# GateLoop attention and a max-out FFN on one core: FFN steps given out whole, none of them between the turn and the cut

## Chip, cores and metric

One core of a Trainium2 chip runs the kernel. The metric is the device time in microseconds (us) of one execution, and the median over several executions is what is compared. Beside it, one execution is recorded by the hardware profiler, which gives a trace of every instruction. TensorE is called PE below, VectorE DVE, ScalarE ACT, GpSimd POOL and SyncE SP, as in the profile.

## What is computed

Two blocks follow each other. The first is attention with a complex gate for each channel (4 batches, 8 heads, 768 positions, 48 channels for each head), written as a recurrence over positions. The second is a feed-forward network over the 3072 tokens that takes the largest of three products.

```python
mag = np.sqrt(a_re * a_re + a_im * a_im)
scale = np.minimum(mag, 0.999) / (mag + 1e-06)
a_re_n, a_im_n = (a_re * scale, a_im * scale)
...
for t in range(S):
    new_re = ar * S_re - ai * S_im
    new_im = ar * S_im + ai * S_re
    S_re, S_im = (new_re + kv, new_im)
    y[:, :, t] = np.einsum('bhd,bhde->bhe', q[:, :, t], S_re)
...
x = attn_out.transpose(0, 2, 1, 3).reshape(B * S, H * D)
h = np.maximum(np.maximum(x @ w1, x @ w2), x @ w3)
return (h @ w_out).astype(np.float32)
```

w1, w2 and w3 are 384 by 768, w_out is 768 by 384, and everything is float32.

## The kernel before

The recurrence is computed in chunks of 64 positions. A tile `x` is 128 positions of one batch (two chunks); there are 24 tiles, six for each batch, and they are taken in groups of two (one tile of each of two batches), so 12 groups. Groups 0 to 5 are the first two batches, 6 to 11 the others.

For one tile the stages are these, by the names that the profile shows:

- gates (`gate_steps`, L359 to L389): logarithm of the gate's size `Ln` and its angle `w`, in three steps on ACT, DVE and POOL, for both tiles of a group at once. L359 and L358 square `ai` and `ar`; L371 makes `Ln`; L376 to L389 make the angle (L382 and L383 multiply `w` on DVE, L381 multiplies `ai` on POOL).
- `products` (L470 to L490): cumulated sums of `Ln` on PE (`sums`), their exponentials on ACT (`En`, `E`), which scale `k` and `q` on POOL (L477) and, with the angles' sines, on DVE (L482, L487); the results are `uk` and `uq`.
- `angles` (L399 to L440): arctangent on ACT, two DVE operations on `w` (L399 with `ar`, L400 with `ai`), cumulated angles on PE (`cs`), sines on ACT.
- `turn(x, "k")` and `turn(x, "q")`: 16 transposes each of 64 rows on PE (`tp`), copied out by ACT (`K` at L501, `Q` at L505).
- `cut(x)`: 32 small matmuls (`F`), exponentiated by ACT into `f`.
- `state(x)`: 64 matmuls (`dk`, only 32 where a batch's sequence ends), and the state `g` is multiplied by `f` and added to `dk` on DVE (L632, L633), once for each of two chunks. At the start of a sequence ACT copies `g` (L630).
- `prep(x, part)`: the scaled copies `Q` (three operations in part 0), `KB`, `QB` and `QG`, all DVE at L533.
- `scores` (`A` and `B` on PE) and `gather` (four DVE picks into `atm` at L579, two ACT copies at L603).
- `outputs(x)`: the attention's output `y` on PE, copied to `xT` by ACT at L658.

The FFN over a group's 256 tokens is done while the next group's attention runs. `up_step` makes three 128-wide blocks of the hidden layer for one of the three weights: nine matmuls, which the profile lists as 18 records since a float32 matmul has two. The first weight's result is copied to `hT` by ACT (L680), the others are taken as a maximum by DVE (L682). `out_step` makes the output of one tile with six matmuls (12 records), copied by ACT to `ot` (L699) and stored by a DMA of SP. One group has six up steps and two out steps.

All PE results go through one PSUM pool of four slots, each of two banks (`banks`); a new tile takes a slot in rotation and waits until the last reader of what was in it is done.

The steps of the FFN stand in a list. Each up step is a list of three parts, and each out step too, and `every_part` joins them to one list of thirds. `group(g)` works through the attention of a group and calls `feed(n)` at several places, which takes the next `n` thirds from that list. In the first turn of a group, `turned(y)` (L813 to L837) turns the group's second tile, and in the second turn, `turned(y + 1)`, the next group's first tile; between `turn(x, "q")` and `cut(x)` stands `feed(1)` at L832. The last step of the group's list is held back for the next group (`held`, L802).

TensorE runs its instructions in the order in which the program issues them from group 2 on: each is chained to the one ahead of it (`chained`; the chain starts at L872). The other engines' order, and that of PE in the first two groups, is set by a scheduler that looks at dependencies and costs. In the start, `weave` (L794) mixes several lists of steps by position.

Of the kernel before, what the change touches and what calls it, by code (L numbers as in the profile page):

```python
# [12 lines left out]
FP = mybir.dt.float32  # L13
# [4 lines left out]
OP = mybir.AluOpType  # L18
# [33 lines left out]
def kernel(  # L52
# [13 lines left out]
    nc = tc.nc  # L66
    B, H, S, D = q.shape
    P = 128
    L64 = 64
    DD = L64 + D  # L70
    DM = H * D
    FF = moe_w1.shape[1]
    KD = DM // P
    KF = FF // P
    C = 2
    W = C * DM
    TG = C * P
    NS = S // P
    NG = B // C * NS
    NX = NG * C  # L80
# [12 lines left out]
    ld2 = ctx.enter_context(tc.tile_pool(name="ld2", bufs=2))  # L93
# [5 lines left out]
    fp2 = ctx.enter_context(tc.tile_pool(name="fp2", bufs=2))  # L99
    psum = ctx.enter_context(tc.tile_pool(name="psum", bufs=4, space=PSUM))  # L100

    T = {}
# [11 lines left out]
    def chained(f):  # L114

        def g(**kw):
            ins = f(**kw)  # L117
            if "chain" in T:
                if T["chain"] is not None:
                    tc.add_manual_dep(ins.ins, T["chain"].ins.name, order, reason="TensorE's order")  # L120
                T["chain"] = ins
            return ins
        return g

    mm, mt = chained(nc.tensor.matmul), chained(nc.tensor.transpose)

    def banks(nm, n=None):

        ps = psum.tile([P, 2, 512], FP, tag="ps", name=nm)
        return ps if n is None else ps.rearrange("p a n -> p (a n)")[:, 0:n]  # L130
# [47 lines left out]
    fs = [const.tile([P, H, 2, NF], FP, name="f%d" % i) for i in range(2)]  # L178
# [98 lines left out]
    ws = [const.tile([P, KD, FF], FP, name="w%d" % i) for i in range(3)]  # L277
    wo = const.tile([P, KF, DM], FP, name="wo")
# [179 lines left out]
    def products(x):  # L458
        g, c = divmod(x, C)

        def s0():


            ps = banks("sums")
            for n, mat in enumerate((mid, rest)):
                for j in range(2):
                    for ch in range(2):
                        r = slice(ch * L64, (ch + 1) * L64)
                        mm(out=ps[j * L64:(j + 1) * L64, ch, n * HC:(n + 1) * HC], lhsT=mat[r],
                           rhs=every(T["Ln", g][r, c * DM:(c + 1) * DM], j), start=True, stop=True)  # L470
            En = T["En", x] = nat2.tile([P, DM], FP, tag="En", name="En")
            act(out=En.rearrange("p (c n) -> p c n", c=2), in_=ps[:, :, HC:2 * HC], func=AF.Exp, scale=-1.0)
            for nm, sg in (("k", 1.0), ("q", -1.0)):
                E = nat2.tile([P, DM], FP, tag="E", name="E")
                act(out=E.rearrange("p (c n) -> p c n", c=2), in_=ps[:, :, 0:HC], func=AF.Exp, scale=sg)
                eng = nc.gpsimd if g > 1 else nc.vector
                eng.tensor_tensor(out=hd(T[nm, x]), in0=E, in1=hd(T[nm, x]), op=OP.mult)  # L477

        def s1():
            for nm in "kq":  # L480
                u = T["U" + nm, x] = us[nm][x % len(us[nm])]
                nc.vector.tensor_tensor(out=sines_of(u), in0=T["CS", x], in1=two(hd(T[nm, x])), op=OP.mult)  # L482

        def s2():

            u = sines_of(T["Uk", x])
            nc.vector.tensor_tensor(out=u, in0=u, in1=two(T["En", x]), op=OP.mult)  # L487

        return s0, s1, s2
# [169 lines left out]


    def up_step(xs, fs, i):

        n, box = len(xs) * P, {}

        def part(j, f):
            xT = T["xT", xs[-1]]
            if f == 0 and i == 0:

                T["hT", xs[-1]] = ld2.tile([P, KF, n], FP, tag="ar", name="hT") if xs[0] == 0 else \
                    fp2.tile([P, KF, n], FP, tag="hT", padded_shape=[P, KF, TG], name="hT")  # L670
            if j == 0:
                box["ps"] = banks("up", len(fs) * n).rearrange("p (f t) -> p f t", t=n)
            for d in range(KD):
                mm(out=box["ps"][:, j], lhsT=ws[i][:, d, f * P:(f + 1) * P], rhs=xT[:, d],
                   start=(d == 0), stop=(d == KD - 1))
            if j < len(fs) - 1:
                return
            dst = T["hT", xs[-1]][:, fs[0]:fs[-1] + 1]
            if i == 0:
                nc.scalar.copy(out=dst, in_=box["ps"])  # L680
            else:
                nc.vector.tensor_tensor(out=dst, in0=dst, in1=box["ps"], op=OP.max)  # L682

        return [call(part, j, f) for j, f in enumerate(fs)]

    def out_step(xs, x):

        box = {}

        def part(j):  # L690
            hT, o = T["hT", xs[-1]], (x - xs[0]) * P
            if j == 0:
                box["ps"] = banks("op", DM)
            for f in (2 * j, 2 * j + 1):
                mm(out=box["ps"], lhsT=hT[:, f, o:o + P], rhs=wo[:, f], start=(f == 0), stop=(f == KF - 1))
            if j < KF // 2 - 1:
                return
            ot = fp2.tile([P, DM], FP, tag="ot", name="ot")
            nc.scalar.copy(out=ot, in_=box["ps"])  # L699
            t0 = x // C // NS * C * S + x % C * S + x // C % NS * P  # L700
            nc.sync.dma_start(out=out[t0:t0 + P, :], in_=ot)

        return [call(part, j) for j in range(KF // 2)]


    def call(f, *a):
        return lambda: f(*a)

    def pre_steps(g, *meanwhile):
        if g >= NG:  # L710
            return []
        cs = list(range(C))
        parts = [products(g * C + c) for c in cs]
        return gate_steps(g, cs) + [p[0] for p in parts] + [call(angles, g, cs, *meanwhile)] + [p[1] for p in parts]

    def tokens(x):

        return [x] if x < C else [x // C * C + c for c in range(C)]

    def ffn_steps(xs):  # L720

        n = 2 if xs[0] == 0 else 3
        return [up_step(xs, range(f, f + n), i) for f in range(0, KF, n) for i in range(3)] \
            + [out_step(xs, x) for x in xs]

    def every_part(steps):

        return [part for step in steps for part in step]

    def front(x):  # L730
        if x >= NX:
# [55 lines left out]
    for i in range(3, len(blocks)):  # L787
        if i > 3:
            rounds.append(call(weight_round, i))
        for n in range(7, len(blocks)):  # L790
            if n > 7 and n - (4 if n < 9 else 3) == i:
                rounds.append(call(weight_load, n))
    ffn = ffn_steps([0])
    weave((0.0, 1.0, tile_steps(0) + tile_steps(1)), (0.0, 0.7, rounds), (0.15, 0.58, pre_steps(1)),  # L794
          (0.415, 0.44, every_part(ffn[:6])), (0.55, 0.75, every_part(ffn[6:9])), (0.25, 0.27, [call(load, 1, load_v)]), (0.6, 0.62, [call(load, 2, load_a)]),
          (0.75, 1.0, gate_steps(2, list(range(C)))))
    load(2, load_kq)

    held = every_part(ffn[9:])  # L802

    def group(g):
        x, y = g * C, g * C + 1
        load(g + 1, load_v)
        if g > 1:
            load(g + 2, load_a, load_kq)
        ffn = held + every_part(ffn_steps(tokens(x - 1)))
        held[:] = ffn[-3:]  # L810
        del ffn[-3:]

        def feed(n):  # L813

            for _ in range(min(n, len(ffn))):
                ffn.pop(0)()

        pre = pre_steps(g + 1, lambda n: feed(3 * n)) if g + 1 < NG else [lambda: None] * 8
        gates, sums, (turning,), units = pre[:3], pre[3:5], pre[5:6], pre[6:]
        later = gate_steps(g + 2, list(range(C)))[:2] if g + 2 < NG else []  # L820

        def pairs(x):
            for f in (scores, gather):
                for nm in "AB":
                    f(x, nm)

        def turned(x):

            if x < NX:
                turn(x, "k")  # L830
                turn(x, "q")
                feed(1)  # L832
                cut(x)
            state(x - 1)
            if x < NX:
                products(x)[2]()
                prep(x, 0)  # L837

        def rest(x):
            if x < NX:  # L840
                for p in range(1, 4):
                    prep(x, p)

        if g > 1:
            feed(3)
        pairs(x)
        if g > 1:
            gates[2]()
        feed(3)
        if g == 1:  # L850
            load(g + 2, load_a, load_kq)
        turned(y)
        sums[0]()
        sums[1]()
        feed(2)
        outputs(x, tokens(x))
        rest(y)
        turning()
        pairs(y)
        units[0]()  # L860
        units[1]()
        for f in later:
            f()
        feed(6)
        turned(y + 1)
        feed(2)
        outputs(y, tokens(y))
        rest(y + 1)
        feed(len(ffn))

    for g in range(1, NG):
        if g == 2:  # L872
            T["chain"] = None
        group(g)
    for f in held + every_part(ffn_steps(tokens(NX - 1))):
        f()


# [28 lines left out]
```

## Time and profile before

| | |
|---|---|
| median of three executions | 674.94 us (674.42 to 676.21) |
| profiled execution | 676.21 us |
| its span, first to last instruction | 674.5 us |
| PE busy | 588.4 us |
| DVE busy | 479.0 us |
| ACT busy | 405.8 us |
| POOL busy | 122.1 us |
| mean granted TensorE clock | 0.956 |
| PE up records, busy in all | 301.0 us, 1404 of them |
| PE op records, busy in all | 101.3 us, 288 of them |

The page's tenths show the span in 40 slices of 16.9 us each. In the first nine slices (to about 150 us) PE is between 1 and 9 tenths busy while weights and the first tiles are made; from then to the end it is near 9 or above. DVE falls off after slice 36 and ACT too, since the attention is done then and only the FFN of the last group remains. In the rows of a timeline the columns are the start and the duration in us, the engine, the line, the operation, the tile written and those read, the shapes, the number of instructions, and in brackets the idle time ahead of it with what ended it.

### The profile page before, as it was taken

Reading aid. Unit: us, or ns where it says so; the run is one execution under the profiler, and the core shown is the slowest. Engines: PE = TensorE matmul, PEld = TensorE weight load, DVE = VectorE, ACT = ScalarE, POOL = GpSimd, SP = SyncE. Lnnn points to the kernel's source line nnn. Section 1 sums busy time; section 2 is a strip of 40 time slices with the busy share of each in tenths; the row PEclk is TensorE's granted clock in tenths of the full one; section 3 lists DMA queues with packets and bytes.
Section 4 is the critical chain, followed back from the end, with each engine's and each line's share of the span. In section 5 each row is a group of like instructions: output and inputs, shape, how many; then the busy total and the mean of one; then the engine's idle time right before and its main releaser. Section 6 shows DMA issues by size and latency. Waiting matters only on the chain.

```text
span 674.5 us, 22805 instructions
## 1 busy us (share of the span) xinstructions
PE 588.4 (87%) x10076; PEld 469.5 (70%) x10076; DVE 479.0 (71%) x638; ACT 405.8 (60%) x670; POOL 122.1 (18%) x131
## 2 busy tenths in 40 slices
PE   1243767898999999999999999999999999999997
PEld 1132755776777877867867867877777877878785
DVE  3899996885877877877876787787777677555111
ACT  6889687586485576576667665755755854631000
POOL 9300102303212113112014013023023023000000
PEclk9656898898999999999999999999999999999999
DMA  6975632330331330330330420420420210000000
GB/s 133 272 162 137 152 65 57 61 58 17 60 61 26 60 64 22 60 71 16 71 64 23 74 50 14 87 48 25 78 56 14 40 46 3 2 26 3 13 13 24
DMA packets 136547, 39.26 MB, mean 58 GB/s; under 512 B 129152, under 2 KB 132224, under 8 KB 136448
## 3 DMA queue, kind: packets, MB, share of 16 engines
q1 hardware_dynamic: 136448, 37.80, 26.0%
q8 instruction: 79, 1.29, 0.8%
q14 instruction: 20, 0.16, 0.1%
HBM read 33.03 MB, written 4.72 MB: 56 GB/s over the span
## 4 chain that ended last, share of the span: by engine, by line
PE 44%; ACT 28%; DVE 16%; issue 7%; DMA 2%; SPq 1%; POOL 1%; DVEq 0%; POOLq 0%; ACTq 0%
PE up L117 25%; PE op L117 9%; DVE Q L533 6%; ACT f L112 5%; PE y L117 3%; PE A L117 2%; ACT Q L505 2%; ACT CS L112 2%; ACT K L501 2%; PE cs L117 2%; ACT e L112 2%; ACT L133 2%; DVE g L633 2%; DVE g L632 2%; ACT L L112 1%
## 5 line engine op out<-in xcount | busy, mean ns | idle before, releaser
L117 PE MATMUL up<-xT,w 128*128 128x256 f32 (+1 forms) x1404 | 301.0, 371 | 12.8 <-DVE g L633 7.9
L117 PEld LDWEIGHTS up<-xT,w 128*128 128x128 f32 x1404 | 249.3, 192 | 48.6 <-DVE g L633 9.2
L533 DVE TENSOR_TENSOR Q<-Q,f 112x512 f32<-112x512 f32 (+2 forms) x72 | 85.3, 1192 | 59.1 <-ACT f L112 59.1
L117 PE MATMUL op<-wo,hT 128*128 128x384 f32 x288 | 101.3, 497 | 0.2 <-DVE hT L682 0.2
L117 PEld LDWEIGHTS op<-wo,hT 128*128 128x128 f32 x288 | 52.3, 190 | 32.7 <-DVE hT L682 0.8
L682 DVE TENSOR_TENSOR hT<-hT,up 128x768 f32<-128x768 f32 (+2 forms) x54 | 46.4, 859 | 39.1 <-PE up L117 39.0
L680 ACT COPY hT<-up 128x768 f32<-128x768 f32 (+2 forms) x27 | 19.6, 727 | 89.5 <-PE up L117 89.1
L381 POOL TENSOR_TENSOR ai<-ai,L 128x768 f32<-128x768 f32 x10 | 22.2, 2222 | 278.8 <-ACT L L112 222.1
L117 PE MATMUL A<-Q,K 112*32 112x80 f32 x1536 | 35.3, 250 | 13.4 <-DVE Q L533 13.4
L117 PEld LDWEIGHTS A<-Q,K 112*32 112x32 f32 x1536 | 30.5, 119 | 22.8 <-issue 8.7
L117 PE MATMUL y<-atm,vb 128*32 128x64 f32 x1152 | 40.7, 224 | 1.6 <-issue 1.6
L117 PEld LDWEIGHTS y<-atm,vb 128*32 128x32 f32 x1152 | 32.9, 112 | 11.0 <-issue 10.2
L112 ACT ACTIVATE f<-F 48x280 f32<-48x280 f32 x96 | 38.3, 399 | 3.5 <-PE F L117 2.7
L632 DVE TENSOR_TENSOR g<-g,f 112x384 f32<-112x384 f32 x40 | 39.7, 993 | 1.0 <-ACT g L630 1.0
L117 PE MATMUL y<-QG,g 112*32 112x64 f32 x1408 | 39.4, 221 | 0.7 <-ACT g L630 0.3
L477 POOL TENSOR_TENSOR k<-E,k 128x384 f32<-128x384 f32 x20 | 25.1, 1255 | 65.4 <-ACT E L112 65.4
L117 PE MATMUL sums<-Ln,mid 64*64 64x192 f32 x192 | 14.8, 369 | 25.2 <-DVE Ln L371 22.6
L117 PEld LDWEIGHTS y<-QG,g 112*32 112x32 f32 x1408 | 35.1, 110 | 2.0 <-DVE g L633 1.3
L389 POOL TENSOR_TENSOR ai<-ai,carry 1x768 f32<-1x768 f32 x10 | 18.6, 1863 | 96.2 <-DMA ai<-in_a_im_dram 46.9
L477 POOL TENSOR_TENSOR q<-E,q 128x384 f32<-128x384 f32 x20 | 35.2, 1761 | 0.0
L117 PE MATMUL cs<-w,upto 128*64 128x192 f32 x192 | 20.8, 364 | 15.4 <-DVE w L400 15.4
L112 ACT ACTIVATE E<-sums 128x384 f32<-128x384 f32 x48 | 22.2, 491 | 18.9 <-POOL q L477 13.3
(103 smaller groups left out, 926.6 us busy)
## 6 DMA issues: line engine op xcount, KB each, us to landing
ar<-in_a_re_dram SPq DMA_DIRECT2D x24, 192.0 KB
ai<-in_a_im_dram SPq DMA_DIRECT2D x24, 192.0 KB
k<-in_k_dram SPq DMA_DIRECT2D x96, 48.0 KB
q<-in_q_dram SPq DMA_DIRECT2D x96, 48.0 KB
vb<-in_v_dram SPq DMA_DIRECT2D x96, 48.0 KB
out_dram<-ot SPq DMA_DIRECT2D x24, 192.0 KB
raw<-in_moe_w_dram SPq DMA_DIRECT2D x5, 768.0 KB
w<-in_moe_w_dram SPq DMA_DIRECT2D x2, 768.0 KB
```

The lines of the kernel that those rows point to most:

```text
L112: tab(nc.scalar.activation(**kw))
L117: ins = f(**kw)
L133: tab(nc.scalar.preload_act_table_set(nm))
L381: (nc.gpsimd if g > 1 else nc.vector).tensor_tensor(out=ai, in0=ai, in1=L, op=OP.mult)
L389: nc.gpsimd.tensor_tensor(out=ai[0:1], in0=ai[0:1], in1=T["carry", g], op=OP.subtract)
L477: eng.tensor_tensor(out=hd(T[nm, x]), in0=E, in1=hd(T[nm, x]), op=OP.mult)
L501: nc.scalar.copy(out=T["K", x][0:DD].rearrange("p n (j t) -> p j n t", j=2), in_=src)
L505: nc.scalar.copy(out=T["Q", x][0:DD, :, 0:32].rearrange("p (n j a) t -> p j n a t", n=H, j=2), in_=src.rearrange("p j n (a t) -> p j n a t ...
L533: nc.vector.tensor_tensor(out=out, in0=in_, in1=f.to_broadcast([DD, 2 * H - g, n, 8]), op=OP.mult)
L632: nc.vector.tensor_tensor(out=new, in0=four(G[0:DD, c]), in1=F[:, c].to_broadcast([DD, 2, 4, D]), op=OP.mult)
L680: nc.scalar.copy(out=dst, in_=box["ps"])
L682: nc.vector.tensor_tensor(out=dst, in0=dst, in1=box["ps"], op=OP.max)
```

## The change

The steps of the FFN are given out whole. `up_step` and `out_step` run all of their matmuls and the copy at once, `ffn_steps` returns a list of calls, and `every_part` is gone. The counts of `feed` are divided by three, and the `feed(1)` between `turn(x, "q")` and `cut(x)` is gone. Since a turn's third and the two thirds behind it (`feed(2)`) are one step, that whole step now stands behind `sums` in the first turn and behind `state` in the second. The order of all other steps in the program stays. The list that `weave` mixes in the start has whole steps in it as well.

```diff
     def up_step(xs, fs, i):
-        n, box = len(xs) * P, {}
-        def part(j, f):
-            xT = T["xT", xs[-1]]
...
-            if j == 0:
-                box["ps"] = banks("up", len(fs) * n).rearrange("p (f t) -> p f t", t=n)
+        xT, n = T["xT", xs[-1]], len(xs) * P
...
+        ps = banks("up", len(fs) * n).rearrange("p (f t) -> p f t", t=n)
+        for j, f in enumerate(fs):
             for d in range(KD):
-                mm(out=box["ps"][:, j], lhsT=ws[i][:, d, f * P:(f + 1) * P], rhs=xT[:, d],
-                   start=(d == 0), stop=(d == KD - 1))
-            if j < len(fs) - 1:
-                return
...
+                mm(out=ps[:, j], lhsT=ws[i][:, d, f * P:(f + 1) * P], rhs=xT[:, d],
+                                 start=(d == 0), stop=(d == KD - 1))
+        if i == 0:
+            nc.scalar.copy(out=dst, in_=ps)
+        else:
+            nc.vector.tensor_tensor(out=dst, in0=dst, in1=ps, op=OP.max)
-        return [call(part, j, f) for j, f in enumerate(fs)]
...
     def out_step(xs, x):
-        def part(j):
-            hT, o = T["hT", xs[-1]], (x - xs[0]) * P
-            if j == 0:
-                box["ps"] = banks("op", DM)
-            for f in (2 * j, 2 * j + 1):
-                mm(out=box["ps"], lhsT=hT[:, f, o:o + P], rhs=wo[:, f], start=(f == 0), stop=(f == KF - 1))
-            if j < KF // 2 - 1:
-                return
...
+        ps = banks("op", DM)
+        for f in range(KF):
+            mm(out=ps, lhsT=hT[:, f, o:o + P], rhs=wo[:, f], start=(f == 0), stop=(f == KF - 1))
...
-        return [up_step(xs, range(f, f + n), i) for f in range(0, KF, n) for i in range(3)] \
-            + [out_step(xs, x) for x in xs]
-    def every_part(steps):
-        return [part for step in steps for part in step]
+        return [call(up_step, xs, range(f, f + n), i) for f in range(0, KF, n) for i in range(3)] \
+            + [call(out_step, xs, x) for x in xs]
...
-          (0.415, 0.44, every_part(ffn[:6])), (0.55, 0.75, every_part(ffn[6:9])), (0.25, 0.27, [call(load, 1, load_v)]), (0.6, 0.62, [call(load, 2, load_a)]),
+          (0.415, 0.44, ffn[:6]), (0.55, 0.75, ffn[6:9]), (0.25, 0.27, [call(load, 1, load_v)]), (0.6, 0.62, [call(load, 2, load_a)]),
...
-    held = every_part(ffn[9:])
+    held = ffn[9:]
...
-        ffn = held + every_part(ffn_steps(tokens(x - 1)))
-        held[:] = ffn[-3:]
-        del ffn[-3:]
+        ffn = held + ffn_steps(tokens(x - 1))
+        held[:] = [ffn.pop()]
...
-        pre = pre_steps(g + 1, lambda n: feed(3 * n)) if g + 1 < NG else [lambda: None] * 8
+        pre = pre_steps(g + 1, feed) if g + 1 < NG else [lambda: None] * 8
...
             if x < NX:
                 turn(x, "k")
                 turn(x, "q")
-                feed(1)
                 cut(x)
             state(x - 1)
...
         if g > 1:
-            feed(3)
+            feed(1)
         pairs(x)
         if g > 1:
             gates[2]()
-        feed(3)
+        feed(1)
...
         turned(y)
         sums[0]()
         sums[1]()
-        feed(2)
+        feed(1)
         outputs(x, tokens(x))
...
-        feed(6)
+        feed(2)
         turned(y + 1)
-        feed(2)
+        feed(1)
         outputs(y, tokens(y))
         rest(y + 1)
         feed(len(ffn))
...
-    for f in held + every_part(ffn_steps(tokens(NX - 1))):
+    for f in held + ffn_steps(tokens(NX - 1)):
         f()
```

More of the change, by code (lines that the diff above doesn't have):

```diff
@@ L661, in up_step @@
     def up_step(xs, fs, i):
-        n, box = len(xs) * P, {}
-        def part(j, f):
-            xT = T["xT", xs[-1]]
-            if f == 0 and i == 0:
-                T["hT", xs[-1]] = ld2.tile([P, KF, n], FP, tag="ar", name="hT") if xs[0] == 0 else \
-                    fp2.tile([P, KF, n], FP, tag="hT", padded_shape=[P, KF, TG], name="hT")
-            if j == 0:
-                box["ps"] = banks("up", len(fs) * n).rearrange("p (f t) -> p f t", t=n)
-            for d in range(KD):
-                mm(out=box["ps"][:, j], lhsT=ws[i][:, d, f * P:(f + 1) * P], rhs=xT[:, d],
-                   start=(d == 0), stop=(d == KD - 1))
-            if j < len(fs) - 1:
-                return
[L678 to L682, printed above, removed]
@@ L684, in up_step @@
-        return [call(part, j, f) for j, f in enumerate(fs)]
-    def out_step(xs, x):
-        box = {}
-        def part(j):
-            hT, o = T["hT", xs[-1]], (x - xs[0]) * P
-            if j == 0:
-                box["ps"] = banks("op", DM)
-            for f in (2 * j, 2 * j + 1):
-                mm(out=box["ps"], lhsT=hT[:, f, o:o + P], rhs=wo[:, f], start=(f == 0), stop=(f == KF - 1))
-            if j < KF // 2 - 1:
-                return
[L698 to L703, printed above, removed]
+        xT, n = T["xT", xs[-1]], len(xs) * P
@@ new lines, in up_step @@
+        if fs[0] == 0 and i == 0:
+            T["hT", xs[-1]] = ld2.tile([P, KF, n], FP, tag="ar", name="hT") if xs[0] == 0 else \
+                fp2.tile([P, KF, n], FP, tag="hT", padded_shape=[P, KF, TG], name="hT")
+        dst = T["hT", xs[-1]][:, fs[0]:fs[-1] + 1]
+        ps = banks("up", len(fs) * n).rearrange("p (f t) -> p f t", t=n)
+        for j, f in enumerate(fs):
+            for d in range(KD):
+                mm(out=ps[:, j], lhsT=ws[i][:, d, f * P:(f + 1) * P], rhs=xT[:, d],
+                                 start=(d == 0), stop=(d == KD - 1))
@@ new lines, in up_step @@
+        if i == 0:
+            nc.scalar.copy(out=dst, in_=ps)
+        else:
+            nc.vector.tensor_tensor(out=dst, in0=dst, in1=ps, op=OP.max)
+    def out_step(xs, x):
+        hT, o = T["hT", xs[-1]], (x - xs[0]) * P
+        ps = banks("op", DM)
+        for f in range(KF):
+            mm(out=ps, lhsT=hT[:, f, o:o + P], rhs=wo[:, f], start=(f == 0), stop=(f == KF - 1))
+        ot = fp2.tile([P, DM], FP, tag="ot", name="ot")
+        nc.scalar.copy(out=ot, in_=ps)
+        t0 = x // C // NS * C * S + x % C * S + x // C % NS * P
+        nc.sync.dma_start(out=out[t0:t0 + P, :], in_=ot)
```

## The prediction

> **What bounds the kernel now.** I read the page's busy times first, then its chain of waits.
>
> ```profile
> PE 588.4 (87%) x10076; PEld 469.5 (70%) x10076; DVE 479.0 (71%) x638; ACT 405.8 (60%) x670; POOL 122.1 (18%) x131
> ...
> PE 44%; ACT 28%; DVE 16%; issue 7%; DMA 2%; SPq 1%; POOL 1%; DVEq 0%; POOLq 0%; ACTq 0%
> ```
>
> PE is the busiest engine, yet over half of the chain lies elsewhere. So I went by stages. A group (two tiles) ends with the start of its run of 36 up records, called x36 here: 172.42 us in group 2, then 221.95, 271.49, 319.92, 367.42, 416.77, 466.29, 515.81, 565.35, 613.25. A full group takes 49.5 us, and PE is busy 47.98 of them. What PE waits for then is in the waits between 206 and 550 us:
>
> ```profile
> DVE Q L533 <- ACT f L112: 37.3, 14, 3.2
> PE up L117 <- DVE g L633: 5.7, 6, 1.1
> PE dk L117 <- ACT K L501: 1.7, 7, 0.2
> ```
>
> The largest one, about 1 us in each full group, is x36 itself: its PSUM slot was dk's, and DVE's second g add (L633) frees that. Behind this add stands DVE's row from ACT's f. So the end of a full group belongs to a chain over ACT and DVE, with PE some 1 us from being the bound. Group 3 by engines:
>
> ```profile
> 242.12 1.56 PE L117 MATMUL op<-wo,hT 128*128 128x384 f32 x4
> ...
> 244.41 1.14 PE L117 MATMUL dk<-vb,uk 64*64 64x48 f32 x64 [0.24 <-ACT K L501]
> ...
> 256.05 4.15 PE L117 MATMUL up<-xT,w 128*128 128x256 f32 x18
> ...
> 261.17 1.56 PE L117 MATMUL up<-xT,w 128*128 128x256 f32 x6
> ```
>
> ```profile
> 242.36 0.95 DVE L682 TENSOR_TENSOR hT<-hT,up 128x768 f32<-128x768 f32 x1
> ...
> 247.64 0.69 DVE L533 TENSOR_TENSOR Q<-Q,f 112x512 f32<-112x512 f32 x1 [2.60 <-ACT f L112]
> 248.25 0.55 DVE L633 TENSOR_TENSOR g<-g,dk 112x384 f32<-112x384 f32 x1
> 248.72 1.22 DVE L533 TENSOR_TENSOR Q<-Q,f 112x1024 f32<-112x1024 f32 x1
> 249.85 2.17 DVE L632 TENSOR_TENSOR g<-g,f 112x384 f32<-112x384 f32 x1
> ...
> 252.81 0.54 DVE L633 TENSOR_TENSOR g<-g,dk 112x384 f32<-112x384 f32 x1
> ...
> 254.48 0.95 DVE L382 TENSOR_TENSOR w<-w,L 128x768 f32<-128x768 f32 x1
> ```
>
> ```profile
> 255.51 0.84 ACT L359 ACTIVATE L<-ai 128x768 f32<-128x768 f32 x1 [4.65 <-DVE w L382]
> ...
> 260.82 0.80 ACT L680 COPY hT<-up 128x768 f32<-128x768 f32 x1
> ```
>
> **What goes and comes.** Counts stay the same on every engine, and so does every queue of SP and POOL. One third step (six records of up or four of op, 1.39 us alone) leaves the place between the transposes and F in each turn, and is done behind sums or dk with the rest of its step. With it the scheduler changes DVE's and ACT's order, and the PSUM slots go round differently.
>
> **Second turn of a group (241 to 250 us).** The third (242.12) is cover: it hides PE's wait for dk's slot. Without it F runs at 242.1, and dk waits for the slot that the last up step held, which DVE's hT max frees at 243.3: 0.7 us idle, in place of 0.24 for K. The y that follows stood about 0.4 us among its own matmuls (248.58 to 248.85, and in its start) for the g add; in the new order that add is already done. 0.7 + 0.1 against 0.24 + 0.4: +0.1 at most, and f (ACT, 245.98, behind its Q copy) doesn't depend on it. I take 0.
>
> **DVE behind the second turn's f.** The new order puts the first g add ahead of the first Q. It needs only dk, so it runs in DVE's 2.60 us of idleness: 0.46 us off the path. The L632 multiply then runs before POOL's L381 (249.43, 2.17 us), and the big Q and the second add beside it, so that the add falls into what was the stall of 1.62 us, and the last Q waits in the multiply's place. Bounds: the add isn't blocked (it took 0.54 at 270.89 beside POOL's multiply of 270.12): another 0.47; it is blocked: 0. I take the first, since that row has the same operation. Sum 0.47 to 0.94, L382 begins near 253.54.
>
> The Trainium skill ("SBUF — State Buffer", section "Who interferes with whom") gives POOL and DVE one port pair, held for a whole instruction; it blocks a DVE operation with two SBUF inputs. The 2.17 against 0.55 us of L632 agrees; an add with one operand in PSUM is outside that rule, which gives the upper bound too.
>
> **ACT's order there.** In six groups (2, 3, 4, 5, 7, 8) L359, which waits for L382, now stands ahead of the xT copy that the 18 up records wait for. With L382 ended at 254.5, L359 ends at 255.4 and xT at 255.8, before B ends at 256.05: nothing. If DVE gains nothing, xT ends at 256.8 and the up run comes 0.75 late; that cover is thin.
>
> **First turn (256 to 271 us).** With DVE 0.94 ahead, the picks of atm end at 259.1 instead of 259.9, ACT's atm copies follow, and hT's copy is no longer held by ACT's row but by the end of the 18 up records: 260.29 for 260.82, 0.53 sooner. K, Q, f, the Qs and the g add follow it, each behind the other without a pause but f's. F no longer stands behind the third (261.17, 1.56), so it never holds f. PE does F, dk and sums, then the whole step from f's end, 264.46 to 268.55, and y until 270.27; x36 starts at 270.96, still after the add, with 0.7 us idle instead of 1.08. So -0.53 for each interval of full groups. Bounds: 0 (the blocked add, the xT copy late) and -0.94 (DVE's whole gain).
>
> **Sum over the groups.** Intervals 2 to 3, 3 to 4, 7 to 8, 8 to 9, 9 to 10: 5 x -0.53 = -2.65. Interval 4 to 5: -0.1. Interval 5 to 6 has no chunk behind its sequence's last tile: dk takes 0.68 us (342.31), PE waits for nothing but dk's 0.24 and 0.34 at x36, so the lost cover counts: 0.63 before dk and 0.36 for K and Q before the op records, less 0.24 = +0.75. Intervals 6 to 7 and 10 to 11 I put at -0.4 and -0.5 in the same way. Together -2.9. After 613.25 PE works alone, with the same work: 0.
>
> **Before group 2.** Here the third is on the path:
>
> ```profile
> 159.07 0.66 PE L117 MATMUL tp<-ident,uq 64*112 64x64 f32 x16 [1.78 <-DVE atm L579]
> 160.53 2.86 PE L117 MATMUL up<-xT,w 128*128 128x256 f32 x6 [0.80 <-ACT atm L603]
> 163.32 0.86 PE L117 MATMUL F<-cuts,Ln 64*48 64x35 f32 x32
> ...
> 164.25 1.63 ACT L112 ACTIVATE f<-F 48x280 f32<-48x280 f32 x4 [1.13 <-PE F L117]
> ```
>
> F ends too late for f by 1.13 us; without the third, f follows the Q copy (162.10 + 1.03): -1.15. In group 1's first half, F (114.05) waits 0.44 for ACT's ot copy, and everything there is scheduled freely; in the new order DVE does L382 and L383 ahead of two of the picks, L361 earlier, and Ln ahead of KB and QB. The worked gain at f (116.44) is near 2, and I cannot see whether the chain past it keeps it: bounds 0 and -2; half, -1.0.
>
> Sum: -2.9 - 1.15 - 1.0 = -5.0. The profiled execution took 676.21 with a span of 674.5 (1.7 around it), 1.27 above the median. Its span becomes 669.5, and the median 674.94 - 5.0 = 669.9.
>
> **A rule against the change.** The up third at 160.53 took 2.86 us for what takes 1.56 in group 3, at a granted clock of 0.83 between 160 and 170 us, after waits of 1.78 and 0.80 with only transposes between. The Trainium skill ("TensorE: Matmul & The Clock Gate", section "Why this matters for your kernels") warns of gaps above some 3 us; leaving the transposes without matmul work behind them lengthens such a gap. By that rule a run of up records could take 1.3 more wherever it comes.
>
> The groups of this profile, with gaps to 1.08 us, hold a clock of 1.00 (206 to 256 us), so the sum has nothing for it.
>
> **Rivals.** *Only half of it shows* (0.16): either the groups or the early part keeps its gain. For it: early waits are shifted easily, since Ln, POOL and loads meet there. 674.94 - 2.5 = 672.4 (671.5 to 673.4).
> *No change* (0.18): the add is blocked by POOL, ACT's flip eats the rest, and x36 waits as before; only the 1.15 of group 1 stay: 673.8. For it: the thin cover of 0.3 us before B's end. Against it: the 0.54 at 270.89.
> *Lost cover* (0.24): PE, not the chain, ends each group, and what is charged for interval 5 to 6 is charged in all nine: dk's wait for hT max without the repayment at y. 9 x 0.75 = +6.75, and 681.7; less group 1's 1.15, 680.5. It decides once PE's idle time at x36 is used up, 1.08 us in a full group. For it: PE is at 47.98 of 49.5. Against it: in the full groups y repays 0.4, and x36 still waits in my working.
>
> **How the numbers follow.** My forecast has 0.42, with 667.5 to 672.2 for it alone (the bounds of the early part, and of the adds). A measurement of this kernel can tell 0.3% from no change: 672.9 to 677.0 is the same. Faster: 0.42 + half of the first rival 0.10 = 0.52; same: 0.06 + 0.18 = 0.24; slower: 0.24. The range 667 to 680 leaves out a little below and the upper half of the last rival, under 0.2.
>
> **What would show it.** F directly behind the transposes in each turn; dk waiting for DVE's hT by about 0.7 in second turns; the g add ahead of the first Q, and a Q, not L632, stretched to some 2.5 us; L359 ahead of xT and the 18 up records without a wait for xT; x36 to x36 near 49.0 in full groups; x36 of group 2 near 170.3. If x36 comes without waiting for g, or y comes late in every group, PE has become the bound and I am wrong on the side of slower.

## The result, and the profile after

| | before | after |
|---|---|---|
| median | 674.88 us (674.42 to 676.21) | 668.00 us (667.46 to 668.85) |
| profiled execution, its span | 676.21, 674.5 us | 668.43, 666.7 us |
| group 1's `cs` | 80.92 us | 81.16 us |
| from group 1's `cs` to group 3's | 99.46 us | 96.07 us |
| x36 to x36 in a full group | 49.52 us | 48.94 us |
| from group 2's x36 to group 11's | 440.8 us | 436.1 us |
| from group 11's x36 to the end | 61.3 us | 61.3 us |

The ratio is 0.9896, with a 95% interval of 0.9877 to 0.9914: 6.9 us less, where 5.0 were forecast. The 7.8 us by which the two spans differ come in two parts: 3.4 us between group 1's and group 3's `cs` (the cumulated angles; group 3's stand right behind group 2's x36), and 4.6 us from group 2's x36 to group 11's; group 1's `cs` came 0.2 us later. The stretch behind group 11's x36 is the same. Below, `cs` 1, 2 and 3 are those of groups 1 to 3, which the texts from before the runs call the first, the second and the third; group 0's, at 27 us, isn't counted.

The page of the changed kernel, with the busy times (PE's by 6.6 us less, with a mean granted clock of 0.963 for 0.956) and the chain of waits:

```profile
PE 581.8 (87%) x10076; PEld 472.5 (71%) x10076; DVE 476.9 (72%) x638; ACT 404.2 (61%) x670; POOL 122.4 (18%) x131
...
PE 46%; ACT 24%; DVE 16%; issue 8%; DMA 3%; SPq 2%; POOL 1%; DVEq 0%; POOLq 0%; ACTq 0%
```

ACT's share of the chain fell by four points. The waits of the changed kernel between 206 and 550 us (engine and tile, what it waited for, total us, times, longest):

```profile
DVE Q L533 <- ACT f L112: 32.8, 14, 2.8
...
PE dk L117 <- DVE hT L676: 4.8, 7, 0.7
...
PE up L117 <- ACT f L112: 3.4, 7, 0.6
PE up L117 <- DVE g L633: 3.0, 5, 0.6
```

These waits of PE sum up to 11.2 us, more than the 9.4 of before (5.7, 1.7, 1.7 and 0.3), and the time is shorter. They stand at three places: for hT ahead of dk in the second turn, for f ahead of the whole up step in the first, and for the second g add at x36. That last wait was 1.08 us in the kernel before:

```profile
271.49 8.04 PE L117 MATMUL up<-xT,w 128*128 128x256 f32 x36 [1.08 <-DVE g L633]
```

PE's part of one full group's timeline in the changed kernel, start and duration first (the last row is the start of x36):

```profile
238.37 0.56 PE L117 MATMUL F<-cuts,Ln 64*48 64x35 f32 x32
239.62 1.14 PE L117 MATMUL dk<-vb,uk 64*64 64x48 f32 x64 [0.69 <-DVE hT L676]
240.69 4.14 PE L117 MATMUL op<-wo,hT 128*128 128x384 f32 x12
...
252.29 4.15 PE L117 MATMUL up<-xT,w 128*128 128x256 f32 x18
...
257.42 0.56 PE L117 MATMUL F<-cuts,Ln 64*48 64x35 f32 x32
...
260.67 4.15 PE L117 MATMUL up<-xT,w 128*128 128x256 f32 x18 [0.44 <-ACT f L112]
267.15 2.21 PE L117 MATMUL up<-xT,w 128*128 128x256 f32 x9 [0.60 <-DVE g L633]
```

DVE's part, behind the second turn's f, and POOL's multiply beside it:

```profile
241.22 0.55 DVE L633 TENSOR_TENSOR g<-g,dk 112x384 f32<-112x384 f32 x1
243.91 0.69 DVE L533 TENSOR_TENSOR Q<-Q,f 112x512 f32<-112x512 f32 x1 [2.14 <-ACT f L112]
244.51 0.55 DVE L632 TENSOR_TENSOR g<-g,f 112x384 f32<-112x384 f32 x1
244.98 1.22 DVE L533 TENSOR_TENSOR Q<-Q,f 112x1024 f32<-112x1024 f32 x1
246.12 0.55 DVE L633 TENSOR_TENSOR g<-g,dk 112x384 f32<-112x384 f32 x1
246.58 2.10 DVE L533 TENSOR_TENSOR Q<-Q,f 112x768 f32<-112x768 f32 x1
...
249.81 0.95 DVE L382 TENSOR_TENSOR w<-w,L 128x768 f32<-128x768 f32 x1
```

```profile
245.70 2.18 POOL L381 TENSOR_TENSOR ai<-ai,L 128x768 f32<-128x768 f32 x1 [27.14 <-ACT L L112]
```

The first add is done in DVE's idle time. The multiply of L632 takes 0.55 us, not 2.17; the second add takes 0.55 beside POOL's L381 (2.18 us), so it isn't blocked; the last Q waits in their place (2.10). From the first Q to L382 there are 5.90 us, 6.84 before. ACT's part:

```profile
250.84 0.85 ACT L359 ACTIVATE L<-ai 128x768 f32<-128x768 f32 x1 [4.72 <-issue]
251.59 0.46 ACT L658 COPY xT<-y 128x384 f32<-128x384 f32 x1
...
256.48 0.80 ACT L674 COPY hT<-up 128x768 f32<-128x768 f32 x1 [0.35 <-PE up L117]
...
258.98 1.63 ACT L112 ACTIVATE f<-F 48x280 f32<-48x280 f32 x4
```

xT is copied behind L359, and done at 252.05, 0.24 us ahead of the 18 up records. hT's copy follows the end of the up records directly, and f follows Q without a gap.

### The profile page after: what moved, and what is told of

It is laid out like the page before. It is cut to its first block, busy times and chain, and to the rows that moved or that the text cites. A ratio compares the mean times of both kernels' runs of the same rounds, so it can differ in the third digit from the quotient of the medians.

```text
span 666.7 us, 22815 instructions
## 1 busy us (share of the span) xinstructions
PE 581.8 (87%) x10076; PEld 472.5 (71%) x10076; DVE 476.9 (72%) x638; ACT 404.2 (61%) x670; POOL 122.4 (18%) x131
## 4 chain that ended last, share of the span: by engine, by line
PE 46%; ACT 24%; DVE 16%; issue 8%; DMA 3%; SPq 2%; POOL 1%; DVEq 0%; POOLq 0%; ACTq 0%
PE up L117 24%; PE op L117 12%; DVE Q L533 6%; PE y L117 3%; ACT CS L112 3%; ACT f L112 2%; ACT L133 2%; ACT e L112 2%; PE A L117 2%; ACT Q L505 2%; PE cs L117 2%; ACT K L501 2%; PE dk L117 2%; DVE g L632 2%; DMA ai<-in_a_im_dram 1%
## 5 line engine op out<-in xcount | busy, mean ns | idle before, releaser
L117 PE MATMUL up<-xT,w 128*128 128x256 f32 (+1 forms) x1404 | 295.9, 369 | 11.0 <-ACT f L112 4.5
L533 DVE TENSOR_TENSOR Q<-Q,f 112x512 f32<-112x512 f32 (+2 forms) x72 | 91.6, 1278 | 49.2 <-ACT f L112 49.2
L117 PE MATMUL op<-wo,hT 128*128 128x384 f32 x288 | 99.0, 494 | 0.5 <-ACT K L501 0.4
L381 POOL TENSOR_TENSOR ai<-ai,L 128x768 f32<-128x768 f32 x10 | 22.3, 2226 | 276.9 <-ACT L L112 188.0
L487 DVE TENSOR_TENSOR uk<-uk,En 128x768 f32<-128x768 f32 x24 | 24.5, 1021 | 18.0 <-PE tp L117 18.0
L412 DVE SCALAR_TENSOR_TENSOR nf<-t,cs 128x384 f32<-128x384 f32 x24 | 13.3, 554 | 28.5 <-ACT t L410 27.4
```

The lines of the kernel that those rows point to most:

```text
L381: (nc.gpsimd if g > 1 else nc.vector).tensor_tensor(out=ai, in0=ai, in1=L, op=OP.mult)
L533: nc.vector.tensor_tensor(out=out, in0=in_, in1=f.to_broadcast([DD, 2 * H - g, n, 8]), op=OP.mult)
```

## The experiments

In the runs, "full group" is the distance from one x36 to the next where both tiles have two chunks; it repeats to 0.03 us within a profile. "cs 1 to 3" is the start's distance from group 1's `cs` to group 3's, which doesn't repeat so well (96.07 and 96.40 in two profiles of the changed kernel).

| run | ratio to before, 95% | full group, us | cs 1 to 3, us |
|---|---|---|---|
| second_turn_only | 1.0002 [0.9982, 1.0021] | 49.49 | 99.40 |
| first_turn_only | 0.9975 [0.9957, 0.9992] | 49.54 | 99.23 |
| after_adds_in_row | 0.9948 [0.9930, 0.9967] | 49.54 | 96.07 |
| before_adds_first | 0.9971 [0.9958, 0.9985] | 49.26 | 98.87 |
| start_whole_steps | 0.9973 [0.9957, 0.9990] | 49.53 | 96.85 |
| turns_alone | 0.9900 [0.9883, 0.9917] | 48.94 | 97.30 |
| changed_again | 0.9898 [0.9872, 0.9925] | 48.94 | 96.40 |
| cover_in_second | 0.9859 [0.9837, 0.9882] | 48.70 | 96.76 |
| first_turn_adds_first | 0.9827 [0.9801, 0.9853] | 48.28 | 97.04 |
| both_orders | 0.9813 [0.9797, 0.9830] | 48.04 | 96.74 |

### The third out of one turn alone

The kernel before, with `feed(between)` in `turned`, and the third added to the next feed:

```diff
-        turned(y + 1)
-        feed(2)
+        turned(y + 1, 0)
+        feed(3)
```

> The kernel before with the third taken out of the second turn alone (it joins the next two thirds); the first turn keeps its third. DVE's order becomes that of the changed kernel. Theory (both are needed: DVE's adds out of the row behind the second turn's f, so that hT, K and Q are copied sooner in the first turn, and F not behind a third there): hT's copy comes about 0.5 us sooner, but F still ends near 1.5 us behind the transposes and holds f, so a full group stays at 49.4 to 49.5 us and the time at 674 to 675. Rival D (DVE's order alone brings it): full groups of 48.95, time near 671.5. Rival P (the cover on PE is what counts, in the first turn): no gain.

The same for the first turn, `turned(y, 0)` and `feed(3)` behind `sums`:

> The kernel before with the third taken out of the first turn alone; the second turn keeps its third and DVE's order there stays as before. Theory: F is early, but f waits for ACT's Q copy as before, so full groups stay at 49.5; only group 1, where F held f by 1.13 us, gains: 673.5. Rival P: full groups of 48.95 and 670.5. Rival D: as the theory.

Measured: neither gains anything in a full group. Where the third is out of the second turn alone, DVE has the new order, and ACT copies hT at the end of the up records, 259.98 us:

```profile
259.98 0.80 ACT L680 COPY hT<-up 128x768 f32<-128x768 f32 x1 [0.34 <-PE up L117]
...
263.04 1.63 ACT L112 ACTIVATE f<-F 48x280 f32<-48x280 f32 x4 [0.43 <-PE F L117]
```

But f waits for F, which stands behind the first turn's third. Where the third is out of the first turn alone, F is early, and hT's copy late:

```profile
259.86 0.56 PE L117 MATMUL F<-cuts,Ln 64*48 64x35 f32 x32
```

```profile
258.73 0.74 ACT L603 COPY atm<-B 32x256 f32<-32x256 f32 x2 [0.50 <-DVE atm L579]
259.49 0.80 ACT L680 COPY hT<-up 128x768 f32<-128x768 f32 x1
...
262.00 1.64 ACT L112 ACTIVATE f<-F 48x280 f32<-48x280 f32 x4
```

The up records had ended by 258.9, but atm's copies waited for DVE's picks, and hT, K, Q and f stand in a row behind them on ACT. So F's place and DVE's order hold f in turn, and taking away either alone moves f, from one x36, by 0.03 us at most. The 0.25% of first_turn_only isn't in the full groups: the interval from group 10's x36 to group 11's shrank by 0.9 us, which is the edit's. Its group 1's `cs` was 1.1 us earlier in the profile, in a part that doesn't differ from the kernel before, so that is not.

### DVE's order alone

The changed kernel, with one dependency in second turns from group 2 on:

```diff
         turned(y + 1)
+        if g > 1 and ("ga", y, 0) in T and ("ga", y, 1) in T and y + 1 < NX:
+            behind(T["ga", y, 0], T["Q", y + 1, 0][0])
```

(`behind(late, early)` adds an order between two DVE instructions; "ga" and "gm" are the add and the multiply of `state`, "Q" what `prep` makes.)

> The changed kernel with one order set by hand: in second turns from group 2 on the first g add stands behind the first Q again, which gives DVE and ACT the order of the kernel before, with PE's order of the changed kernel. Theory: hT in the first turn is copied as late as before, x36 to x36 is 49.5 again in full groups; what is gained before group 2 (3.2 us) stays, and the interval from group 5 to 6 loses some 0.3: 671.5 to 672. Rival P: full groups of 48.95 and 668, as the changed kernel. Rival D: as the theory.

The kernel before, with the new order by hand:

```diff
         rest(y + 1)
+        if g > 1 and ("ga", y, 0) in T and ("ga", y, 1) in T and y + 1 < NX:
+            first, second, third = T["Q", y + 1, 0]
+            row = [T["ga", y, 0], first, T["gm", y, 1], second, T["ga", y, 1], third, T["Q", y + 1, 1][0], T["Q", y + 1, 2][0], T["Q", y + 1, 3][0]]
+            for early, late in zip(row, row[1:]):
+                behind(late, early)
```

Two more orders keep QG behind L382, and the next multiply of L632 behind QG, as they were.

> The kernel before with all of its thirds, and DVE's order in second turns from group 2 on set by hand as in the changed kernel (first g add, Q, multiply, large Q, second g add, last Q). Theory: hT, K and Q come 0.5 us sooner in the first turn but F behind the third holds f: full groups 49.4, time 674 to 674.6. Rival D: full groups of 48.95, time near 672. Rival P: 674.9.

Measured: with the adds in their old place, the changed kernel has full groups of 49.54, and of the groups' gain from group 2 to group 11 only 1.1 us is left, as much as the last interval gives (the others that differ, 4 to 5, 5 to 6 and 6 to 7, cancel out). That speaks against the rival that the cover on PE is what counts. The order by hand in the kernel before gives 49.26, not the 49.4 of the expectation and not 48.95. All of that gain is in PE's second turn, which the expectation left out: from the transposes to A it takes 12.98 us there, 13.23 before and 13.21 in the changed kernel. The third still covers dk's wait, and y no longer stands still for the g add, so F of the first turn comes 0.25 us sooner.

### The start, and the turns without it

The kernel before, with whole steps in the list that the start mixes, and thirds in the groups:

```diff
-          (0.415, 0.44, every_part(ffn[:6])), (0.55, 0.75, every_part(ffn[6:9])), (0.25, 0.27, [call(load, 1, load_v)]), (0.6, 0.62, [call(load, 2, load_a)]),
+          (0.415, 0.44, [step_of(s) for s in ffn[:6]]), (0.55, 0.75, [step_of(s) for s in ffn[6:9]]), (0.25, 0.27, [call(load, 1, load_v)]), (0.6, 0.62, [call(load, 2, load_a)]),
```

> The kernel before, with whole FFN steps in the list that the start mixes, and thirds with their place between the turns kept in every group. Theory: the 2.05 us that the changed kernel gains between the cumulated angles (cs) of 81 and of 129 us come from the start's list alone: cs to cs 46.7 there for 48.66, full groups 49.53 as before, 672.5 in all. Rival (the third in group 1's own turns brings it): 48.5 between these, 674.5.

The reverse, `turned` without a third in every group, and the start in thirds:

> The kernel before with the thirds taken out of both turns in every group, and the start's list still in thirds: the rest of the change beside the run with whole steps in the start. Theory (the parts are independent): full groups of 48.95, the interval from group 10's 36 up records to group 11's 1.1 us shorter, cs to cs in the start as before or 0.3 less (48.4 to 48.7 and 50.3 to 50.8): 674.9 - 4.7 - 0.3 to 0.6 = 669.5 to 670. Rival (the start's list is needed for the groups' gain, since it sets the phase): 49.5 and 674.

And the changed kernel once more:

> The changed kernel as it is, to see how far the start varies from one execution to another: full groups of 48.94 again to 0.02 us; from the first cs to the third 96.07 in the first profile, and 96 to 97 here by the granted clock between 100 and 170 us; 667.5 to 669.

Measured: the groups behave as the theory has it, 49.53 and 48.94, so the start sets nothing there. The start itself falls against the theory. Its list of whole steps alone brings cs 1 to 3 to 96.85 (the four profiles with the list in thirds and a third left in at least one turn give 98.87 to 99.46), but the turns alone bring it to 97.30, and both together give 96.07 to 97.04 in four profiles. The two gains don't add up, and turns_alone is as fast as the changed kernel, 0.9900 for 0.9898. The medians of whole executions say the same: less what the groups give, the list alone gains 1.8 us, the turns alone 2.1 and both together 2.3, each with an interval of 1.1 to 1.8 us either way. The interval from `cs` 1 to 2 alone was 47.49 with the list alone, not 46.7, and 46.61 and 47.24 in two profiles of the same changed kernel. Which instructions of the start carry the gain stays open.

### What is left, and a faster kernel

The changed kernel's waits name what is next: x36's wait for the second g add (0.60), and dk's for hT (0.69) now that PE's path leads to hT's copy. Two edits, alone and together. In first turns DVE does both adds and the multiply ahead of Q:

```diff
         rest(y)
+        if g > 1:
+            line([T[k, x, c] for k, c in (("ga", 0), ("gm", 1), ("ga", 1)) if (k, x, c) in T]
+                 + T["Q", y, 0] + T["Q", y, 1] + T["Q", y, 2])
...
         turned(y + 1)
+        if g > 1 and ("gm", y, 0) in T:
+            behind(T["gm", y, 0], T["Q", y, 2][0])
```

(The second order keeps the next multiply of L632 behind QB in second turns, as it was.)

> The changed kernel, with DVE's order in first turns from group 2 on set by hand: first g add, multiply, second g add ahead of the three Q (before: Q, add, large Q, multiply, last Q, add). Theory: the 36 up records wait 0.60 us for the second g add because it is last in DVE's row behind f; with it in front they don't wait, and a full group takes 48.35: 9 x 0.6 = 5 us less, 663. Rival (the Qs are late instead, and A in the second half waits for them, or y for QG): no gain, 668.

The third back in second turns only, with the changed kernel's DVE order there by hand (the row of before_adds_first, with its two more orders). It is written as an edit of the kernel before, with whole steps in the start's list:

```diff
-        turned(y)
+        turned(y, 0)
...
-        feed(2)
+        feed(3)
...
-        turned(y + 1)
+        turned(y + 1, 1)
         feed(2)
```

> The changed kernel with the third put back between the turn and the cut in second turns alone, and DVE's order there (adds first) and QG behind L382 set by hand to what the changed kernel has. Theory: with DVE ahead, PE's 0.69 us before dk in the second turn lies on the path to hT's copy; with the third as cover it is 0.24, hT's copy comes up to 0.35 sooner (then ACT's atm copies hold it): full groups of 48.6, and 48.94 less some 0.3 in each: 665 to 666. Rival (dk's wait is paid back by y as in the working of the prediction, so the cover is worth nothing): 48.94 and 668.

Both:

> The kernel of the run with the cover in second turns, with the adds first in first turns as well. Theory: the two gains add up: full groups near 48.0, where PE is busy some 47.5, and 660 to 662. Rival (each shortens the same path): the better of the two alone, 663.

Measured: 48.28, 48.70 and 48.04, which is -0.66, -0.24 and -0.90 to the changed kernel's 48.94. The gains add up. The kernel with both takes 662.54 us (662.36 to 663.04), 0.9813 of the kernel before. DVE in its first turn:

```profile
257.62 0.55 DVE L634 TENSOR_TENSOR g<-g,dk 112x384 f32<-112x384 f32 x1 [0.95 <-PE dk L117]
258.21 0.56 DVE L633 TENSOR_TENSOR g<-g,f 112x384 f32<-112x384 f32 x1
258.80 0.55 DVE L634 TENSOR_TENSOR g<-g,dk 112x384 f32<-112x384 f32 x1
259.29 3.49 DVE L534 TENSOR_TENSOR Q<-Q,f 112x512 f32<-112x512 f32 x3
```

and PE's x36 without a wait, dk's slot being free from 259.3 on:

```profile
265.11 1.13 PE L117 MATMUL up<-xT,w 128*128 128x256 f32 x4
```

The three Q in a row take 3.49 us, and A has them long before it runs. Busy times in one full group of this kernel (length, then PE, PEld, DVE, ACT and POOL, clock, DMA):

```profile
225.00:273.00 48.00, 47.30 (x853) 38.10 (x852) 38.23 (x47) 31.66 (x52) 10.21 (x6) 1.00 0.26 53
```

PE is busy 47.30 of 48.00 us, so a reordering has at most 0.7 us left to find in a group.

## Why the prediction was right, and where its sizes were off

**Second turn: 0.** Right. dk waits 0.69 us for hT (0.7 in the prediction), y doesn't wait, and from the transposes to A it takes 13.21 us for 13.23.

**DVE's order: 0.94.** Right to the hundredth (6.84 to 5.90), by the way that was given: the first add in idle time, the second not blocked by POOL, the stall moved to a Q. after_adds_in_row shows that this order is needed: without it full groups are 49.54 again.

**xT behind L359: nothing.** Right, with 0.24 us of cover, where 0.3 was worked out.

**First turn: -0.53 for each full group.** Right in place, -0.58 in size: x36 waits 0.60, not 0.7. The pair of one-turn runs shows what the prediction joined in one step: hT's copy and F are two holds on f, and taking away one of them alone moves f by 0.03 us at most. DVE's order gains 0.26 by itself where the second turn keeps its cover (before_adds_first), but by way of PE's second turn.

**The other intervals.** The interval from group 5 to 6 was put at +0.75 and measured +0.2: the working counted what is lost at dk and op (0.67 from the transposes to A), but didn't take off the 0.34 us that x36 had waited there, which are gone; from A to x36 it is 0.47 less. From 6 to 7 it was put at -0.4 and measured -0.71. DVE's order has no part in that: after_adds_in_row has -0.72 there, before_adds_first nothing, second_turn_only -0.32 and first_turn_only -0.27. From 10 to 11 it was put at -0.5 and measured -1.1. The rows of ACT's f in group 11, before and then after:

```profile
605.98 1.63 ACT L112 ACTIVATE f<-F 48x280 f32<-48x280 f32 x4 [0.43 <-PE F L117]
```

```profile
598.53 1.63 ACT L112 ACTIVATE f<-F 48x280 f32<-48x280 f32 x4
```

From hT's copy to f there are 3.06 us before and 2.50 after, which is the 0.5 that was forecast; another 0.37 lie between A and B (1.47 us before, 1.10 after), where DVE now makes QB ahead of hT's maximum, and 0.2 ahead of hT's copy. Together the intervals gave -4.6 for -2.9. This is nearly all by which the sum was off.

**The early part: -2.15.** The size came out and the parts didn't, so the fit is luck. The medians give 2.3 us (6.9 less the 4.6 of the groups), with an interval of some 1.2 either way. The 3.4 between `cs` 1 and 3 are from two single profiles, and 1.6 of them aren't the change's: behind 129.58 us the kernel before made `cs` and A in 2.55 and 1.90 us, and the changed kernel in 1.52 and 1.31, but before_adds_first, whose program is that of the kernel before up to there, also took 1.52 and 1.31.

The -1.15 for F at 163.32 (which stands in group 2's first turn; the prediction called it group 1's) is the step that failed. The hold on f was read rightly: from the start of the transposes to f it takes 6.39 us for 7.63 before, and 6.40 in first_turn_only. Counted the same way, x36 comes only 0.33 and 0.25 us sooner. Before, and then after:

```profile
172.42 8.04 PE L117 MATMUL up<-xT,w 128*128 128x256 f32 x36 [1.08 <-DVE g L633]
```

```profile
169.26 8.04 PE L117 MATMUL up<-xT,w 128*128 128x256 f32 x36
```

The sum took f's whole gain to x36. But x36 had waited 1.08 us for DVE's chain, and no more than that could be had from it. It now waits for nothing: PE works without a pause from F on and ends the turn itself, and the work up to x36 took it 11.55 us at the low clock, for 10.81 before. The -1.0 for the start was a half taken between two bounds; the runs give some 2 us for the start's list or for the turns, and no sum of both.

**The rule against the change.** In the groups the changed kernel's granted clock is 1.00; the gap of 0.69 us ahead of dk costs no clock there, as the sum had it. In the start it is 0.80 between 160 and 170 us (0.83 before), but 0.86 between 150 and 160 (1.00 before). The third's place doesn't decide this: start_whole_steps, with its thirds, has 0.82 and 0.84 in the two stretches, and changed_again, without them, 0.95 and 0.88. The slow stretch didn't go with the third either, as the section on the hardware shows.

**The rivals.** "No change" and "lost cover" fall: x36's wait shrank from 1.08 to 0.60, and the cover is worth 0.24 in a full group (cover_in_second), not 0.75, and only because DVE has got ahead: with the adds in their old place first_turn_only has the cover, after_adds_in_row hasn't, and both have 49.54. "Only half of it shows" falls too: the groups kept 4.6 us and the start 2.3.

## What to carry to other kernels

When two engines hold the same instruction in turn, removing either hold can show nothing; test them together, and read for each run which engine the held instruction waits for. In a row of an in-order engine, put first what another engine waits for and what needs no late input: two 0.55 us adds behind three large multiplies cost 0.66 us of a full group here, more than F's place (0.56, from 49.26 to 48.70) or the cover (0.24). A filler on a busy engine is worth what it covers on the path that ends the stage, and that changes as soon as the other engine gets ahead.

## What was not expected of the hardware

The low clock of the start isn't tied to the instructions that ran in it before. Without the third, group 2's first turn has its slow stretch on dk and sums, which took 1.08 and 0.56 us before:

```profile
158.53 1.84 PE L117 MATMUL dk<-vb,uk 64*64 64x48 f32 x62
...
161.41 1.02 PE L117 MATMUL sums<-Ln,mid 64*64 64x192 f32 x8
```

And a part of the start moves from one execution to the next: the granted clock between 130 and 140 us was 0.83 in the profile of the kernel before, and 1.00 in before_adds_first, whose program is the same up to there. Group 1's `cs` stood anywhere from 78.4 to 81.2 us over all profiles. A difference of a microsecond before 170 us in a single profile says little here, while one of 0.05 us between two full groups is sure.
